# A second matrix product cut into seven block products: z = h wo1 on pairs of 512-token blocks, with the gated sums' second half moved into the first gated pair

## The chip, the cores and the metric

The program runs on one core of one Trainium2 chip. The metric is device time in microseconds (us) of one execution. Before the change three runs gave 1319.36, 1319.44 and 1320.01 us, median 1319.44 us.

The engines are named as in the profile: PE is TensorE (matrix products), PEld its weight loads, DVE is VectorE, ACT is ScalarE, POOL is GpSimd, and SP is the engine that issues every DMA of this program.

## The reference, cut to what matters

```python
def _attn_ref(q, k, v):                 # q, k, v: 8 x 8 heads x 576 x 64
    scores = scale * np.matmul(q, k.transpose(0, 1, 3, 2))
    ret = scores * Dmat[None]           # decay, lower triangle
    return np.matmul(ret, v)
def _moe_ref(x, w1, w2, w3, w_out):     # x: 4608 x 512, w1..w3: 512 x 768, w_out: 768 x 512
    h = np.maximum(np.maximum(x @ w1, x @ w2), x @ w3)
    return (h @ w_out)
def _moe2_ref(x, w1, w2, w3, w_out):    # w1, w2: 512 x 1024, w3: 1024 x 1024, w_out: 1024 x 512
    a = x @ w1
    b = x @ w2
    h = a * b @ w3
    return (h @ w_out)
```

The output is `_moe2_ref(_moe_ref(_attn_ref(q, k, v)))` for 4608 tokens.

## The kernel before, in words

Every matrix product is made in three matmuls. A float32 operand is **split** into a rounded half (`copy_r`, on ACT) and the rest (`low`, a subtraction on DVE or POOL), and the product of two split operands is high by high, low by high and high by low. The helper `product` writes these three for each pair of operand pieces into one PSUM bank. A matmul has 128 x 128 weights and up to 512 moving columns.

The stages follow each other on PE:

1. **h** (to 580 us of the trace). Nine blocks of 512 tokens: attention, then `h = max(x w1, x w2, x w3)` with six row groups of 128 (`ps_h`, L416), stored to DRAM in `h_d`. Other weights are turned from float64 words into float32 on the way and parked in DRAM (`wo1_d`, `wp_d`, `wo2_d`, `w3t_d`). What runs when is a list of due times: `when(t, ...)` counts in units of one `ps_h` product, `T_BLK = 18` units make a block, and `t_last` is the start of the ninth block. In that block the next stage's weights are fetched and split.
2. **z = h wo1** (581 to 732 us). Twelve tiles of `N2 = 384` tokens; for each, six pieces of 128 along the inner dimension (`KF1`) by four output groups (`KD`), three matmuls each. `load_h` and `split_h` fetch and split h pieces into `hh` and `hl` (a ring of four, the `low` on DVE and POOL in turn). The four banks of a tile go through `zo` to `z_d`. In `slots` of this loop stand steps of the next stages: `sums_of` makes the seven sums of blocks of the gated weights (`a11` to `s4`) for two operands `i` and two column halves `q`, and `open_34` fetches the weights of stage 3.
3. **w4 = w3 w_out** (732 to 776 us), a weight product. For each of eight output groups `m`, eight pieces `k` into one bank (`ps_w`, L584). `wo2` is wholly resident; the `w3t` pieces come through three buffers `raw34`.
4. **gated** (776 to 1122 us). Six pairs of token tiles; in each, four column blocks `o`, and per column block seven block products on the sums (`X`, `V`, `Y` banks; `snap` copies a bank on ACT, `plus` adds on DVE, `times` multiplies on POOL). Two operand sets `ops[0]` and `ops[1]` serve the pairs in turn; `operands` fetches `zr` and makes the next pair's differences and splits in between.
5. **out** (to 1317 us): the product with w4, also by seven block products.

The order of instructions on an engine is the order in which the code calls them. Each engine takes its own queue strictly in that order; SP too, so a DMA whose buffer is not free yet holds all DMAs behind it.

Of the kernel before, what the change touches and what calls it, by code (L numbers as in the profile page):

```python
# [21 lines left out]
G = H // 2  # L22
# [65 lines left out]
def tile_retention_maxout_bilinear(ctx: ExitStack, tc, a, out):  # L88
# [20 lines left out]
    z_d = [dram.tile([P, KD, N2], F32, name=f"z_d{t}") for t in range(NT // N2)]  # L109
# [103 lines left out]
    def w3_unit(t, j, half):  # L213
# [39 lines left out]
    def x_tiles(t):  # L253
        if t not in xs:
            xs[t] = (x_p.tile([P, G, N1], F32R, tag="xh", name="xh"), x_p.tile([P, G, N1], F32R, tag="xl", name="xl"))
# [199 lines left out]
    def open_z():  # L455
        right.close()
        cv_x.close()
        p = zp["p"] = bx.enter_context(tc.tile_pool(name="zp", bufs=1, side="right"))
        zp["w"] = [(p.tile([P, DM], F32R, name=f"w1oh{k}"), p.tile([P, DM], F32R, name=f"w1ol{k}")) for k in range(KF1)]
# [11 lines left out]
    def get_w1o(k):  # L471
        return splitter(zp["p"], wo1_d[:, k], *zp["w"][k], nc.vector if k % 2 else nc.gpsimd, "wr", 2)

    H_RING, H_AHEAD = 4, 4
    hq = dict(loaded=0, split=0)

    def load_h():
        n = hq["loaded"]
        if n < n2 * KF1:
            hq["loaded"] = n + 1  # L480
            j, k = divmod(n, KF1)
            raw = hq[n] = zp["p"].tile([P, N2], F32, tag="hr", name="hr", bufs=H_AHEAD)
            t0, done = j * N2, 0
            while done < N2:
                blk, off = divmod(t0 + done, N1)
                m = min(N1 - off, N2 - done)
                load(raw[:, done:done + m], h_d[blk][:, k, off:off + m])
                done += m

    def split_h():  # L490
        n = hq["split"]
        if n < n2 * KF1:
            hq["split"] = n + 1
            raw = hq.pop(n)
# [506 lines left out]
```

## Time and profile before

| what | us |
|---|---|
| median of three runs | 1319.44 |
| the profiled execution, device time | 1319.27 |
| its span, first to last instruction | 1317.5 |
| PE busy | 1298.2 |
| stage z on PE, first matmul to the first of w4 | 150.9 |
| stage w4 on PE | 43.6 |
| DVE busy in stage z | 75.8 |
| POOL busy in stage z | 74.3 |

The device time is 1.8 us more than the span. A busy PE in the table is PE with a matmul in its pipe. The views used below are the page's own parts, the instructions of one tile, the chain of work that ended last in order of time, the busy time in stretches, the groups of equal instructions, who waited for whom, the DMA issues and the timeline of one engine. In the timeline a row gives start, duration, engine, line, operation and, in brackets, the idle time before it.

### The profile page before, as it was taken

How to read it: one execution, taken by the hardware profiler on the slowest of the kernel's cores; microseconds unless marked ns; L12 is line 12 of the kernel's file. 1: busy time of each engine (PE TensorE's matmuls, PEld its weight loads, DVE VectorE, ACT ScalarE, POOL GpSimd, SP SyncE). 2: the span in 40 equal slices, each digit the busy share in tenths (PEclk: the TensorE clock that was granted, in tenths of full speed). 3: DMA queues.
4: the chain of work that ended last, by engine and by line, in shares of the span. 5: the costliest groups of instructions: out<-in, count | busy, mean ns of one | idle time of the engine just before them, and what ended most of it. 6: DMA issues, size and time to landing. Idle time of an engine off the chain costs nothing.

```text
span 1317.5 us, 24536 instructions
## 1 busy us (share of the span) xinstructions
PE 1298.2 (99%) x9464; PEld 1185.1 (90%) x9464; DVE 757.7 (58%) x1134; ACT 448.5 (34%) x878; POOL 402.2 (31%) x356
## 2 busy tenths in 40 slices
PE   7999999999999999999999999999999999999998
PEld 5888888888888878889999899999999999999998
DVE  5995656766668575227644334334333437788885
ACT  3541212222222122114434333333333324455553
POOL 2111111111111110026634334333433434544443
PEclk9999999999999999999999999999999999999999
DMA  9964768877779885237557432222222222544552
GB/s 219 246 141 97 178 154 211 203 192 192 194 174 188 166 177 132 92 104 226 182 185 235 145 123 85 72 79 74 89 97 79 72 94 73 179 154 152 167 157 93
DMA packets 347748, 193.53 MB, mean 147 GB/s; under 512 B 243056, under 2 KB 321392, under 8 KB 347632
## 3 DMA queue, kind: packets, MB, share of 16 engines
q1 hardware_dynamic: 347632, 191.97, 53.9%
q8 instruction: 74, 1.21, 0.4%
q14 instruction: 42, 0.34, 0.1%
HBM read 125.85 MB, written 66.06 MB: 146 GB/s over the span
## 4 chain that ended last, share of the span: by engine, by line
PE 88%; SPq 6%; DMA 3%; issue 1%; DVE 1%; POOL 0%; ACT 0%; DVEq 0%; POOLq 0%; ACTq 0%
PE ps_h L416 30%; PE ps_x L584 23%; PE ps_y L584 11%; PE ps_z L584 9%; SPq L99 6%; PE ps_v L584 6%; PE ps_w L584 3%; PE o L334 2%; PE sc L321 2%; PE st L346 1%; PE o L340 1%; DMA kn<-in_k_dram 1%; DMA z_d<-zo 0%; DMA w<-w_d 0%; DMA raw<-in_moe_w_dram 0%
## 5 line engine op out<-in xcount | busy, mean ns | idle before, releaser
L416 PE MATMUL ps_h<-xh,w1h 128*128 128x512 f32 (+1 forms) x664 | 259.1, 392 | 0.6 <-ACT hb L93 0.5
L416 PE MATMUL ps_h<-xh,w1l 128*128 128x512 f32 (+1 forms) x664 | 254.6, 385 | 0.4 <-DVE w1l L96 0.2
L416 PE MATMUL ps_h<-xl,w1h 128*128 128x512 f32 (+1 forms) x664 | 174.1, 384 | 0.0
L416 PEld LDWEIGHTS ps_h<-xh,w1h 128*128 128x128 f32 x664 | 124.6, 188 | 30.9 <-issue 3.6
L416 PEld LDWEIGHTS ps_h<-xh,w1l 128*128 128x128 f32 x664 | 124.7, 188 | 24.7 <-DVE w1l L96 0.7
L416 PEld LDWEIGHTS ps_h<-xl,w1h 128*128 128x128 f32 x664 | 123.0, 188 | 24.8
L310 POOL TENSOR_TENSOR v<-v,tables 128x512 f32<-128x512 f32 x40 | 44.5, 1113 | 327.6 <-DMA v<-in_v_dram 306.6
L426 DVE TENSOR_TENSOR hb<-ps_h,hb 128x512 f32<-128x512 f32 (+1 forms) x110 | 74.4, 677 | 112.4 <-PE ps_h L416 104.6
L880 POOL TENSOR_TENSOR c<-c 128x384 f32<-128x384 f32 x72 | 81.7, 1134 | 175.4 <-DVE c L748 87.5
L743 ACT ACTIVATE snap<-ps_x 128x384 f32<-128x384 f32 x120 | 58.5, 492 | 190.7 <-PE ps_x L584 188.5
L584 PE MATMUL ps_z<-hh,w1oh 128*128 128x384 f32 x288 | 96.3, 334 | 0.8 <-issue 0.8
L584 PE MATMUL ps_z<-hl,w1oh 128*128 128x384 f32 x288 | 96.4, 335 | 0.6 <-DVE hl L96 0.6
L584 PE MATMUL ps_z<-hh,w1ol 128*128 128x384 f32 x288 | 96.2, 334 | 0.0
L158 ACT ACTIVATE e<-raw 128x512 f32<-128x512 f32 x64 | 42.8, 669 | 154.4 <-DMA raw<-in_moe_w_dram 96.9
L93 ACT ACTIVATE hb<-ps_h 128x512 f32<-128x512 f32 (+1 forms) x56 | 32.5, 580 | 176.4 <-PE ps_h L416 176.4
L96 POOL TENSOR_TENSOR hl<-hr,hh 128x384 fp32r<-128x384 f32 x36 | 39.4, 1093 | 78.0 <-ACT hh L93 74.2
L748 DVE TENSOR_TENSOR c<-ps_v,snap 128x384 f32<-128x384 f32 x48 | 26.6, 557 | 61.6 <-PE ps_v L584 39.6
L307 POOL TENSOR_TENSOR q<-q,tables 128x512 f32<-128x512 f32 (+1 forms) x31 | 32.0, 1032 | 94.3 <-DMA q<-in_q_dram 76.4
L328 DVE TENSOR_TENSOR p<-sc,tables 128x512 f32<-128x512 f32 (+1 forms) x80 | 47.1, 628 | 18.6 <-PE sc L321 18.6
L93 ACT ACTIVATE hh<-hr 128x384 fp32r<-128x384 f32 x72 | 36.1, 522 | 56.9 <-PE ps_z L584 30.5
L584 PEld LDWEIGHTS ps_z<-hh,w1oh 128*128 128x128 f32 x288 | 54.1, 188 | 1.2 <-issue 1.2
L584 PEld LDWEIGHTS ps_z<-hl,w1oh 128*128 128x128 f32 x288 | 54.1, 188 | 1.1 <-DVE hl L96 1.1
(215 smaller groups left out, 3360.0 us busy)
## 6 DMA issues: line engine op xcount, KB each, us to landing
g_d<-c SPq DMA_DIRECT2D x96, 192.0 KB, 1.9
raw<-in_moe_w_dram SPq DMA_DIRECT2D x34, 512.0 KB, 5.8
h_d<-hb SPq DMA_DIRECT2D x54, 256.0 KB, 3.1
gr<-g_d SPq DMA_DIRECT2D x12, 1024.0 KB, 6.2
z_d<-zo SPq DMA_DIRECT2D x12, 768.0 KB, 3.6
zr<-z_d SPq DMA_DIRECT2D x48, 192.0 KB, 3.3
out_dram<-ob SPq DMA_DIRECT2D x36, 256.0 KB, 2.0
v<-in_v_dram SPq DMA_DIRECT2D x32, 256.0 KB, 4.7
```

The lines of the kernel that those rows point to most:

```text
L93: nc.scalar.activation(dst, src, AF.Copy)
L96: eng.tensor_tensor(dst, full, hi.bitcast(F32), ALU.subtract)
L99: nc.sync.dma_start(out=dst, in_=src)
L158: nc.scalar.activation(z["e"], raw[:, :, 1].bitcast(F32), AF.Copy, scale=2.0 ** -112)
L307: nc.gpsimd.tensor_tensor(z["q"][:, :r], z["q"][:, :r], qs[:, j, :r].unsqueeze(3).to_broadcast([P, r, G, 32]), ALU.mult)
L310: nc.gpsimd.tensor_tensor(z["v"], z["v"], vd.unsqueeze(2).to_broadcast([P, H, D]), ALU.mult)
L328: nc.vector.tensor_tensor(z[g][:c, :, :c], z["sc"][g][:c, :, :c], mask[:c, :c].unsqueeze(1).to_broadcast([c, G, c]), ALU.mult)
L416: nc.tensor.matmul(ps[:, cols], l, r, start=n == 0, stop=n == len(mms) - 1)
L426: nc.vector.tensor_tensor(hb, ps[:, cols], hb, ALU.max)
L584: nc.tensor.matmul(ps, l, r, start=start and j == 0, stop=stop and j == len(mms) - 1, skip_group_check=again)
L743: nc.scalar.activation(t, ps[:, :N2], AF.Copy)
L880: nc.gpsimd.tensor_tensor(x, x, y, ALU.mult)
```

## The change

**z by seven block products.** Tokens are taken in pairs of 512-token blocks (`z_groups`: four pairs, and the ninth block as two halves of 256). The output's four groups are two halves, the inner dimension's six pieces are two halves of three (`KH`). The seven sums of wo1's blocks are made in the ninth block by `z_weights`, from two loads per piece. The differences of the four blocks of h are made per group on DVE (`sub_h`), on 1536 columns at once, and each of the seven resulting operands is split whole: one ACT copy and one DVE subtraction of 1536 columns. Before, each split was of 384 columns. Sums of products leave PSUM through `zs` (ACT) and a DVE addition into `zo`, and `z_d` now holds pairs of tiles.

**The gated sums.** Only half `q = 0` is made beside z, all its `low` on DVE; half `q = 1` is made in the first two column blocks of the first gated pair (`more`, called by `tick`). That pair makes the next pair's operands in its last two column blocks instead of in all four.

**w4.** The loop now runs over `k` outside, with eight banks open; `wo2` is no longer resident but comes through `raw34` too, one piece for every two of `w3t`. The `low` of w3t is on DVE alone, that of wo2 on DVE and POOL in turn.

Places of tiles: `x` has one pool per block; the second half of the gated sums lies on the right side. The transposed w3 is stored in rows of 512 elements.

```diff
-        zp["w"] = [(p.tile([P, DM], F32R, name=f"w1oh{k}"), p.tile([P, DM], F32R, name=f"w1ol{k}")) for k in range(KF1)]
+        zp["w"] = {x: [p.tile([P, KH, half], F32R, name=f"z{x}{v}") for v in "hl"] for x in AN}
...
+    Z_ORDER = (("a11", "b11"), ("a12", "b21"), ("s2", "t2"), ("s1", "t1"), ("s3", "t3"), ("s4", "b22"), ("a22", "t4"))
+    Z_RING = 3
+    z_groups = [(2 * j, 2 * j + 1, 0, N1) for j in range(n_blk // 2)] + [(n_blk - 1, n_blk - 1, N1 // 2, N1 // 2)]
...
+    def sub_h(eng, j, dst, x, y, tag=None):
+        if j < len(z_groups):
+            r = hr[j, dst] = raw_h(tag)[:, :, :z_groups[j][3]] if tag else hr[j, x if x[0] == "b" and dst == "t1" else y]
+            eng.tensor_tensor(r, hr[j, x], hr[j, y], ALU.subtract)
...
+    def split_h(n):
+        j, n = divmod(n, len(Z_ORDER))
+        if j < len(z_groups):
+            x = Z_ORDER[n][1]
+            raw, size = hr[j, x], z_groups[j][3]
+            hh, hl = hq[j, n] = [zp["p"].tile([P, KH, N1], F32R, tag=f"h{v}", name=f"h{v}", bufs=Z_RING)[:, :, :size] for v in "hl"]
             copy_r(hh, raw)
-            low(nc.vector if n % 2 else nc.gpsimd, hl, raw, hh)
+            low(nc.vector, hl, raw, hh)
...
+        behind_z = {0: [(h_t4, 0)], 1: [(load_h, 1, "b12")], 2: [(load_h, 1, "b21")], 3: [(h_t3, 1), (load_h, 2, "b22")],
+                    4: [(h_t1, 1)], 5: [(h_t2, 1), (load_h, 2, "b11")], 6: []}
+        for j, (_, _, _, size) in enumerate(z_groups):
...
+            for n, (x, y) in enumerate(Z_ORDER):
+                bank_of = "XVXYXYX"[n]
...
+                for i in range(2):
+                    ms = slice(i * P, i * P + P)
+                    product(ps[i][:, :size], [(ah[:, c, ms], al[:, c, ms], bh[:, c], bl[:, c]) for c in range(KH)], fresh, True, not fresh)
+                for i in range(2):
+                    if n in (0, 2, 3):
+                        saved[n, i] = snap_z(ps[i], size)
+                    elif n == 6:
+                        keep_z(j, 2 + i, 0, ps[i])
+                    else:
+                        keep_z(j, *{1: (i, 0), 4: (2 + i, 1), 5: (i, 1)}[n], ps[i], saved.pop(({1: 0, 4: 3, 5: 2}[n], i)))
+                split_h(j * len(Z_ORDER) + n + Z_RING)
+                for fn, dj, *args in behind_z[n]:
+                    fn(j + dj, *args)
+                if steps and n in (2, 3, 5, 6):
                     steps.pop(0)()
...
-        for m in range(KF2):
-            th, tl = w3t.pop(m)
-            ps = bank8("ps_w")
-            product(ps, [(th[:, k], tl[:, k], oh[k], ol[k]) for k in range(KF2)])
...
+        for n in range(2 * KF2):
+            k, e = divmod(n, 2)
+            th, tl = w3t.pop(n)
+            for m in range(4 * e, 4 * e + 4):
+                if k == 0:
+                    ps_w.append(bank8(f"ps_w{m}"))
+                product(ps_w[m], [(th[:, m % 4], tl[:, m % 4], *wo2[k])], k == 0, k == KF2 - 1)
...
+            prepare_34(*[(get_w3t, n + 3)] * (n + 3 < 2 * KF2), *[(get_wo2, k + 2)] * (e == 1 and k + 2 < KF2))
...
+        more = in_turn([sums_of(i, 1, lambda: mp, 2, (nc.vector, nc.vector)) for i in range(2)])
+        more.pop(0)()
...
+                if p == 0 and o == 2:
+                    for step in steps:
+                        step()
+                    open_second()
+                    a1, b1 = (operands(1, ops[1], c) for c in range(2))
+                    steps = [a1[0], waiting, waiting, *a1[1:], b1[0], waiting, *b1[1:]]
```

In stage z, DVE's queue held before, around the end of a tile, splits of 384 columns (`hl`), the gated weights' sums (`s3`, `s4` and their rest) and copies out of PSUM (`zo`):

```order
L96 TENSOR_TENSOR hl_6697<-hr_6607,hh_6696 128x384
L96 TENSOR_TENSOR hl_6741<-hr_6656,hh_6740 128x384
L558 TENSOR_TENSOR s3_6748<-a00_6466,a10_6470 128x512
L631 COPY zo_6750<-ps_z_6619 128x384
L631 COPY zo_6750<-ps_z_6621 128x384
L96 TENSOR_TENSOR hl_6791<-hr_6700,hh_6790 128x384
L96 TENSOR_TENSOR s2l10_6310<-s2_6682,s2h10_6309 128x512
```

Now, behind the fourth, fifth and sixth product of the first group, it holds splits of 1536 columns, the next group's differences (`T3`, `b12`, `T2`), gated sums and additions out of PSUM:

```order
L96 TENSOR_TENSOR hl_6481<-T2_6236,hh_6480 128x1536
L522 TENSOR_TENSOR T3_6484<-b22_6163,b12_6418 128x1536
L96 TENSOR_TENSOR a22l00_6330<-a11_6454,a22h00_6329 128x512
L606 TENSOR_TENSOR a11_6454<-a10_6452,a11_6454 128x512
L676 TENSOR_TENSOR zo_6509<-ps_X0_6359,zs_6476 128x512
L676 TENSOR_TENSOR zo_6513<-ps_X1_6360,zs_6478 128x512
L96 TENSOR_TENSOR hl_6518<-b11_6277,hh_6517 128x1536
L522 TENSOR_TENSOR b12_6418<-b12_6418,b11_6277 128x1536
L676 TENSOR_TENSOR zo_6540<-ps_Y0_6456,zs_6438 128x512
L676 TENSOR_TENSOR zo_6544<-ps_Y1_6457,zs_6440 128x512
```

All of h's splits and differences have moved to DVE, four times as wide, and POOL has none of them left.

SP's queue in stage w4 was, before, pairs of w3t loads with a store of a finished bank between them:

```order
L99 DMA raw34_8044<-w3t_d_61 128x512
L99 DMA raw34_8046<-w3t_d_61 128x512
L99 DMA w4_d_97<-w4_8048 128x512
L99 DMA raw34_8089<-w3t_d_61 128x512
L99 DMA raw34_8091<-w3t_d_61 128x512
L99 DMA w4_d_97<-w4_8093 128x512
```

Now there is a wo2 load among every two of w3t, all through the same three buffers, and the stores come at the stage's end:

```order
L99 DMA raw34_7552<-w3t_d_61 128x512
L99 DMA zr_7554<-z_d0_73 128x768 x2
L99 DMA raw34_7577<-w3t_d_61 128x512
L99 DMA raw34_7581<-wo2_d_60 128x512
L99 DMA raw34_7601<-w3t_d_61 128x512
L99 DMA raw34_7623<-w3t_d_61 128x512
L99 DMA raw34_7627<-wo2_d_60 128x512
```

Three loads now belong to 24 matmuls of PE, where two did.

In the first column block of the first gated pair, DVE's queue was, before, the additions out of PSUM (`c`) with a difference now and then:

```order
L748 TENSOR_TENSOR c_8366<-ps_v0_8334,snap_8350 128x384
L748 TENSOR_TENSOR c_8368<-ps_v1_8335,snap_8352 128x384
L748 TENSOR_TENSOR c_8421<-ps_x0_8332,snap_8399 128x384
L748 TENSOR_TENSOR c_8423<-ps_x1_8333,snap_8401 128x384
L678 TENSOR_TENSOR t_8428<-zr_8403 128x384
```

Now six operations of the gated sums stand between the first two pairs of additions:

```order
L830 TENSOR_TENSOR c_7970<-ps_v1_7937,snap_7954 128x384
L96 TENSOR_TENSOR a22l01_7488<-a11_7932,a22h01_7487 128x512
L606 TENSOR_TENSOR a11_7932<-a10_7930,a11_7932 128x512
L96 TENSOR_TENSOR a11l01_7484<-a00_7926,a11h01_7483 128x512
L606 TENSOR_TENSOR a10_7930<-a00_7926,a10_7930 128x512
L96 TENSOR_TENSOR s1l01_7490<-a11_7932,s1h01_7489 128x512
L606 TENSOR_TENSOR a00_7926<-a11_7932,a00_7926 128x512
L830 TENSOR_TENSOR c_8035<-ps_x0_7934,snap_8007 128x384
```

The second pair of additions, which PE needs before its seventh product, has moved behind them.

## Rows read from the trace of the kernel before

**Rows 1.** The page, busy time by engine, and by slice PE and its clock.

```profile
PE 1298.2 (99%) x9464; PEld 1185.1 (90%) x9464; DVE 757.7 (58%) x1134; ACT 448.5 (34%) x878; POOL 402.2 (31%) x356
...
PE   7999999999999999999999999999999999999998
...
PEclk9999999999999999999999999999999999999999
```

**Rows 2.** Who waited for whom on PE: us in total, times, longest.

```profile
PE ps_x L584 <- DVE c L748: 2.4, 1, 2.4
...
PE ps_z L584 <- issue: 0.8, 1, 0.8
```

**Rows 3.** Tiles ps_z and ps_w: ns min/median/max of one, first and last start.

```profile
L584 PE MATMUL ps_z<-hh,w1oh x288: 334/334/414, 581.4 to 731.8; 128*128 128x384 f32 x144
...
L584 PE MATMUL ps_w<-oh,th x64: 387/389/393, 732.3 to 775.2; 128*128 128x512 f32 x64
```

**Rows 4.** The chain in order of time: start, us, what and how many.

```profile
609.80 122.67 PE ps_z L584 x706
732.47 43.56 PE ps_w L584 x192
...
780.28 2.12 PE ps_x L584 x12
...
839.57 2.08 PE ps_x L584 x12
...
1190.88 2.85 PE ps_x L584 x24
```

**Rows 5.** Busy time in the stretches of z and w4: length, then engine by engine.

```profile
581.40:732.30 150.90, 150.33 (x864) 149.78 (x865) 75.82 (x88) 65.08 (x132) 74.25 (x60) 1.00 0.61 195
733.00:775.00 42.00, 42.00 (x187) 34.75 (x186) 18.16 (x19) 16.68 (x33) 19.23 (x16) 1.00 0.55 176
```

**Rows 6.** Timeline of DVE in the ninth block and at the start of z.

```profile
545.28 0.69 DVE L426 TENSOR_TENSOR hb<-ps_h,hb 128x512 f32<-128x512 f32 x1 [4.80 <-PE ps_h L416]
545.89 0.68 DVE L96 TENSOR_TENSOR w1ol<-wr,w1oh 128x512 fp32r<-128x512 f32 x1
...
581.20 0.55 DVE L96 TENSOR_TENSOR hl<-hr,hh 128x384 fp32r<-128x384 f32 x1
```

**Rows 7.** Timeline of DVE and of POOL in stage w4.

```profile
739.29 1.26 DVE L96 TENSOR_TENSOR tl<-raw,th 128x512 fp32r<-128x512 f32 x1 [6.22 <-ACT th L93]
...
738.71 1.29 POOL L96 TENSOR_TENSOR tl<-raw,th 128x512 fp32r<-128x512 f32 x1 [13.86 <-ACT th L93]
```

**Rows 8.** ACT's copies by form: busy, mean ns of one, idle before.

```profile
L93 ACT ACTIVATE hb<-ps_h 128x512 f32<-128x512 f32 x52 | 30.9, 595 | 173.1 <-PE ps_h L416 173.1
...
L93 ACT ACTIVATE hh<-hr 128x384 fp32r<-128x384 f32 x72 | 36.1, 522 | 56.9 <-PE ps_z L584 30.5 <-DMA hr<-h_d 10.3 <-issue 8.7
```

**Rows 9.** DMA issues, 733 to 765 us: count, KB each, median us to landing.

```profile
raw<-w3t_d SPq DMA_DIRECT2D x12, 256.0 KB, 4.0
```

**Rows 10.** DMA issues of the whole run, the same columns.

```profile
raw<-in_moe_w_dram SPq DMA_DIRECT2D x34, 512.0 KB, 5.8
...
gr<-g_d SPq DMA_DIRECT2D x12, 1024.0 KB, 6.2
...
a<-wp_d SPq DMA_DIRECT2D x16, 256.0 KB, 4.4
...
raw<-wo_d SPq DMA_DIRECT2D x8, 256.0 KB, 3.3
```

**Rows 11.** The gated stage's additions on DVE and multiplications on POOL, by form.

```profile
L880 POOL TENSOR_TENSOR c<-c 128x384 f32<-128x384 f32 x72 | 81.7, 1134 | 175.4 <-DVE c L748 87.5 <-issue 51.8 <-PE ps_x L584 21.2
...
L748 DVE TENSOR_TENSOR c<-ps_v,snap 128x384 f32<-128x384 f32 x48 | 26.6, 557 | 61.6 <-PE ps_v L584 39.6 <-ACT snap L743 22.0
```

More of the change, by code (lines that the diff above doesn't have):

```diff
@@ L469, in splitter @@
         return split
[L471 to L488, printed above, removed]
@@ L510, in tile_retention_maxout_bilinear @@
-    for n in range(2):
-        when(t_last + 15 + n, split_h)
+    for c, tag in enumerate(("T3", "T2", "b21")):
+        for n, step in enumerate(z_weights(c, tag)):
+            when(t_last + 0.5 + 3 * c + (1.2 + 0.35 * n if n else 0), step)
+    for n, x in enumerate(("b12", "b22", "b11")):
+        when(t_last + 1 + 2 * n, load_h, 0, x)
+    when(t_last + 10.5, load_h, 0, "b21")
+    when(t_last + 9, load_h, 1, "b22")
+    for n, fn in enumerate((h_t3, h_t1, h_t2)):
+        when(t_last + 9.5 + 1.6 * n, fn, 0)
@@ L513, in tile_retention_maxout_bilinear @@
+    for n in range(Z_RING):
+        when(t_last + 13.6 + n, split_h, n)
+    when(t_last + 15.2, load_h, 1, "b11")
     with tc.manual_schedule():
@@ new lines, in snap_z, with keep_z @@
+        def snap_z(ps, size):
+            t = zo_p.tile([P, N1], F32, tag="zs", name="zs", bufs=6)[:, :size]
+            nc.scalar.activation(t, ps[:, :size], AF.Copy)
+            return t
+        def keep_z(j, m, n, ps, other=None):
+            t, off, size = z_groups[j][n], n * z_groups[j][2], z_groups[j][3]
+            o = zo_p.tile([P, N1], F32, tag="zo", name="zo", bufs=4)[:, :size]
+            if other is None:
+                nc.scalar.activation(o, ps[:, :size], AF.Copy)
+            else:
+                nc.vector.tensor_tensor(o, ps[:, :size], other, ALU.add)
+            at0, done = t * N1 + off, 0
+            while done < size:
+                pair, to = divmod(at0 + done, 2 * N2)
+                part = min(2 * N2 - to, size - done)
+                load(z_d[pair][:, m, to:to + part], o[:, done:done + part])
+                done += part
@@ L862, in next_steps, with tick @@
             def next_steps(n):
-                for _ in range(n if p + 1 < n_pair or o < 1 else 2 * n):
+                for _ in range(0 if p == 0 else n if p + 1 < n_pair or o < 1 else 2 * n):
+                    if steps:
+                        steps.pop(0)()
+            def tick(n=1):
+                for _ in range(n if p == 0 else 0):
                     if steps:
```

239 lines of the change are left out of this document (133 added, 106 removed).

## The prediction

> **What bounds the kernel now.** I read the page first: PE is busy 1298.2 of 1317.5 us, in nine tenths or more of every slice but the first and the last, at a granted clock of nine tenths or more, which is the 2.4 GHz level [rows 1]. So time is PE's, and anything else counts only where PE waits for it. PE's waits are few: the longest beside the start is 2.4 us, and in stage z the gap at its beginning of 0.8 us [rows 2]. Then I read the stage that changes. Its first matmul starts at 581.4 us and the first of w4 at 732.3 us, so z holds PE for 150.9 us [rows 3]. In it DVE is busy for 75.8 us and POOL for 74.3 us of 150.9 us [rows 5]: half idle, and off the path. A second is thus gained where PE has fewer columns to stream, and lost where an engine that was half idle becomes late.
>
> **PE's work in z.** From the chain, 706 matmuls of 384 columns take 122.67 us, 0.1738 us each; 192 of 512 columns take 43.56 us, 0.2269 us each; 24 of 256 columns take 2.85 us, 0.1188 us each [rows 4]. Before, 12 tiles x 6 pieces x 4 groups x 3 matmuls = 864 of 384 columns: 150.1 us, and 150.9 us as measured, with the small gaps. After, a group has 7 products x 2 halves x 3 pieces x 3 matmuls = 126. Four groups are of 512 columns (504 matmuls, 114.3 us) and one of 256 (126 matmuls, 15.0 us). The sum is 129.3 us. PE loses **21.6 us** of work.
>
> The rows let the size be checked. 384, 512 and 256 columns at 2.4 GHz are 160, 213.3 and 106.7 ns; each row is 12 to 14 ns above. The Trainium skill, "TensorE: Matmul & The Clock Gate", section "Wait — 56ns, not 53.3ns?", has a fixed cost of about 2.5 ns per warm matmul; with it the gain would be 17.9 us as an estimate (41,472 columns fewer, and 234 matmuls fewer at 2.5 ns). The rows above don't agree with so small a cost.
>
> **What feeds z.** Each full group lasts 126 x 0.2269 = 28.6 us, a product 4.08 us. Does DVE keep up, now that POOL has no part in it? No row has an operation of 1536 columns. The rest of a split takes 0.55 us for 384 columns and 0.68 us for 512, and the next operation follows 0.61 us after the start of one of 512 [rows 6]. So 128 columns cost 0.13 us, 1536 columns 0.68 + 8 x 0.13 = 1.72 us; three spacings of 0.61 us, 1.83 us, bound it from above. I take 1.7 us. A group has 7 rests and 4 differences (18.7 us), 6 additions out of PSUM (3.7 us at 0.61), and a quarter of the 22 operations of the gated sums (3.4 us): 25.8 of 28.6 us. It fits, at nine tenths. ACT has per group 7 copies of 1536 columns, 8 of 512 and some of the sums; with 0.52 us for 384 and 0.60 for 512 [rows 8] one of 1536 is about 1.2 us, and the sum about 17 us.
>
> The load is uneven: behind products 4, 5 and 6 DVE has 4.6, 4.6 and 5.8 us of work in 4.08 us, and 2.9 to 3.3 us behind the others. Its worst lag is so some 2.7 us, plus 1.2 to 2 us for ACT's copy ahead of the rest. A split is made two products (8.2 us) before PE needs it, so nothing is late here, by some 2 us. The weights' 33 operations of 256 columns and the first differences fall into the ninth block, where DVE is busy one operation in 2.7 us. **Start of z: 0**, with the old gap of 0.8 us staying.
>
> The h loads are of 768 KB; the nearest rows are 512 KB in 5.8 us and 1024 KB in 6.2 us [rows 10]. Each is issued at least 7 us before its use, b12 the closest; I take 0 for them.
>
> The last group of 256 columns runs at 2.14 us a product. Behind its fourth product two rests of w4's weights wait on a DMA of 256 KB (4.0 us in the next stage, [rows 9]), and the additions that free X for the seventh product stand behind them on DVE. **0.3 us**, bounds 0 and 2.
>
> **w4.** PE's 192 matmuls stay. But three buffers now carry three loads per 5.45 us of PE (24 matmuls) instead of two. A buffer's round is landing 4.0 us [rows 9], ACT's copy 0.6 us, and the rest on POOL 1.3 us or on DVE 0.7 to 1.3 us (1.26 beside a busy POOL, [rows 7]): 5.3 to 5.9 us. At 5.9 it slips 0.45 us in each of seven rounds, 3.2 us, of which a lead of some 1.2 us at the start takes its part: **2.0 us**. Lower bound 0 (loads in 3.3 us [rows 10], round 4.6); upper 12.6 us (loads in the 5.8 us of the 512 KB row, round 7.7 us at POOL's price and 7.3 at DVE's, so some 2 us in each of seven rounds, less the lead).
>
> **First gated pair.** A column block takes 7 x 2.12 = 14.84 us of PE [rows 4]. DVE has in it 7 additions at 0.56 us [rows 11] and now 11 operations of the sums at 0.61 us, 10.6 us; where POOL runs one of its three multiplications (1.13 us, [rows 11]) DVE's own stands still, as the 1.26 us for 0.68 show [rows 7]: up to 3.4 us more, 14.0 us. In the first block the sums also wait for their load, issued after w4's stores and 4.4 us on its way [rows 10], some 2.6 us beyond their place. The lag of 1.8 us reaches the bank that the next block's second product needs: **1.2 us**, bounds 0 and 5.8 (all 22 operations at 1.26 us). The next pair's operands, squeezed into two blocks, have their DMA started 4 us or more ahead: 0.
>
> One more thing has a price but no direction. Twelve matmuls take 2.12 us in the pairs with one operand set and 2.08 us in those with the other [rows 4], and the moved half of the sums changes which tiles meet. Six of 24 blocks may gain 0.28 us each, six may lose as much: 0, bounds -1.7 and +1.7 us.
>
> What hides at nothing: ACT's copies, z's stores (256 KB where they were 768 KB, as many bytes), and the moved load steps on SP.
>
> **Sum.** 1319.27 - 21.6 + 0.3 + 2.0 + 1.2 = **1301.2 us**. That is against the profiled execution, which is 0.17 us under the median.
>
> **Rivals.**
> - *DVE becomes the bound of z.* It does from (28.6 - 7.1) / 11 = 1.95 us per operation of 1536 columns. At 2.1 us a group takes 30.2 us, the stage 137 us, the total about 1309 us. For it: DVE is at nine tenths, and the same operation took 1.26 us beside POOL [rows 7]. Against it: POOL has nothing in this stage.
> - The Trainium skill, "VectorE: DVE Perf Modes", sections "The TRN2 errata" and "The DRAIN you can't avoid", has (N + 151) / 0.96 ns for an fp32 addition and no overlap of one operation with the next: as an estimate 1.76 us for 1536 columns and 27.3 us a group, still under 28.6. The duration agrees with the 0.68 us row, the spacing of 0.61 us doesn't.
> - *The same, and slower than before.* The five groups then take over 150.9 us, from 4 (11p + 7.1) + 5.5p + 5.5 = 150.9, p = 2.36 us. At the stretched price of 1.26 us per 512 columns, 3.8 us, a group takes 49 us and the total is near 1386 us. What decides is whether DVE streams 1536 columns of two SBUF operands as freely as 512.
> - *w4's buffers*: the upper bound above, about 1312 us.
> - *Matmuls at 2.5 ns over their columns*, a gain of 17.9 us only: 1305 us.
> - *The change doesn't do what it says*: excluded for PE's part, since its queue is 234 matmuls shorter in the order of instructions.
>
> **How the numbers follow.** Forecast 77% (1296 to 1306); w4's buffers 8% (1306 to 1314); DVE as bound, still faster, 6% (1304 to 1316); smaller gain per matmul 3%; slower 4%; something that leaves it within 0.2% of before, 2%. The range 1296 to 1310 leaves out the upper parts of the second and third and the last two, less than 2 in 10. About 0.2%, 2.6 us, is what a measurement of this kernel can tell from no change. Faster 94%, same 2%, slower 4%.
>
> **What would show it.** In the changed profile: z's matmuls at 0.227 us each from about 581 to 711 us, 630 of them, with no wait on DVE's `hl`; DVE's operations of 1536 columns at 1.7 us (wrong from 1.95); w4 at 43.6 us plus some 2 us of waits for `tl` or `ol`; a wait of PE in the first gated pair on DVE's `c`, once or twice; all pairs from the second on as before. A w4 stage over 50 us would prove the buffers' rival, a group over 29 us DVE's.

## The result, and the profile after

| | before | after |
|---|---|---|
| device time, median of four runs, us | 1319.72 | 1297.42 (1295.95 to 1300.0) |
| the profiled execution: device time, span | 1319.27, 1317.5 | 1296.76, 1294.8 |
| ratio after to before | | 0.9828, 95% interval 0.9807 to 0.9850 |

The forecast was 1301.2 us in a range from 1296 to 1310 us. The time lies in the range, 3.8 us under the forecast. The profiled execution is 0.7 us faster than the median; its profile tells where the forecast and the time part. The page of the changed kernel answers to [rows 1]:

```profile
PE 1274.6 (98%) x9230; PEld 1141.9 (88%) x9230; DVE 828.0 (64%) x1217; ACT 474.6 (37%) x872; POOL 323.2 (25%) x289
...
PEclk9999999999999999999999999999999999999999
```

PE has 234 matmuls fewer, is busy 23.6 us less (1298.2 before), and still sets the time; its granted clock is at the 2.4 GHz level in every slice. DVE has 70 us more to do than before, POOL 79 us less. The busy time in the stretches of z, w4, and the first half and the second half of the first gated pair (length, then PE, PEld, DVE, ACT, POOL, clock, DMA share, GB/s) answers to [rows 5]:

```profile
580.60:710.10 129.50, 129.50 (x630) 109.68 (x631) 106.16 (x104) 71.00 (x88) 0.00 (x0) 1.00 0.51 169
710.10:754.40 44.30, 43.83 (x194) 35.99 (x193) 22.70 (x29) 22.27 (x42) 16.25 (x13) 1.00 0.61 192
754.40:784.90 30.50, 30.24 (x170) 29.57 (x170) 21.13 (x35) 15.15 (x31) 7.76 (x7) 1.00 0.41 136
784.90:814.00 29.10, 29.10 (x169) 29.10 (x169) 14.88 (x25) 11.66 (x27) 15.20 (x14) 1.00 0.34 116
```

Stage z holds PE for 129.5 us instead of 150.9 us [rows 3], with no idle in it. DVE is busy in 106 of 129.5 us where it was in 76 of 150.9. In the third row PE is short of its stretch by 0.3 us, in w4 by 0.5 us. The chain in order of time (start, us, what, how many) gives the pitches, as [rows 4] did:

```profile
633.97 8.16 PE ps_X L637 x36
642.13 4.08 PE ps_V L637 x18
...
699.48 2.16 PE ps_X L637 x18
...
776.32 2.12 PE ps_y L637 x12
...
787.13 2.08 PE ps_v L637 x12
...
876.67 2.12 PE ps_x L637 x12
...
906.27 2.08 PE ps_x L637 x12
```

A product of 18 matmuls of 512 columns takes 4.08 us, 226.7 ns each; one of 256 columns takes 2.16 us, 120.0 ns each. In the gated stage a pair that uses the first operand set (776, 876 us) begins at 2.12 us per twelve matmuls and goes on at 2.08 us (787, 906 us): its last two column blocks, whose sums the change has moved to the right side, run faster. Before, all four ran at 2.12 us.

By PE's own stage boundaries, in us (the last column is a second execution of the changed kernel, of the run "changed" below):

| stage | before | after | second execution |
|---|---|---|---|
| z starts at | 581.4 | 580.6 | 582.4 |
| z | 150.9 | 129.5 | 129.8 |
| w4 | 43.6 | 44.3 | 44.1 |
| gated, 23 of 24 column blocks | 338.8 | 337.8 | 338.7 |
| last block and out | 199.4 | 199.2 | 199.1 |

So of 22.7 us of span, 21.4 are z's, w4 gives 0.8 back, the gated stage gains 1.7 by its pitch and loses 0.8 in the first pair, and h and the end have 1.1 us less. The second execution gains less (1299.4 us of device time): h is 1.0 us longer there than before, and the first pair loses 1.6 us.

### The profile page after: what moved, and what is told of

Its sections match the earlier page's. It is cut to its first block, busy times and chain, and to the rows that moved or that the text cites. A ratio compares the mean times of both kernels' runs of the same rounds, so it can differ in the third digit from the quotient of the medians.

```text
span 1294.8 us, 23828 instructions
## 1 busy us (share of the span) xinstructions
PE 1274.6 (98%) x9230; PEld 1141.9 (88%) x9230; DVE 828.0 (64%) x1217; ACT 474.6 (37%) x872; POOL 323.2 (25%) x289
## 4 chain that ended last, share of the span: by engine, by line
PE 95%; DVE 2%; DMA 1%; issue 1%; ACT 0%; POOL 0%; SPq 0%; POOLq 0%; DVEq 0%; ACTq 0%
PE ps_h L417 34%; PE ps_x L637 23%; PE ps_y L637 11%; PE ps_X L637 6%; PE ps_v L637 5%; PE ps_Y L637 3%; PE ps_w L637 3%; PE o L335 3%; PE sc L322 3%; PE st L347 2%; PE ps_V L637 1%; PE o L341 1%; DMA w<-w_d 0%; DMA a<-wp_d 0%; DMA q<-in_q_dram 0%
## 5 line engine op out<-in xcount | busy, mean ns | idle before, releaser
L311 POOL TENSOR_TENSOR v<-v,tables 128x512 f32<-128x512 f32 x40 | 44.3, 1107 | 322.6 <-DMA v<-in_v_dram 311.4
L96 POOL TENSOR_TENSOR ol<-raw,oh 128x512 fp32r<-128x512 f32 x4 | 5.6, 1408 | 216.6 <-DMA z_d<-zo 212.7
L165 DVE CUSTOM_DVE_ANT_0 m<-m,r 128x1024 uint16<-128x1024 uint16 x64 | 51.4, 804 | 7.0 <-ACT r L160 0.2
L830 DVE TENSOR_TENSOR c<-ps_x,snap 128x384 f32<-128x384 f32 x48 | 25.4, 552 | 43.6 <-PE ps_x L637 43.6
L169 DVE SCALAR_TENSOR_TENSOR w<-raw,m 128x512 int32<-128x512 int32 x64 | 49.4, 774 | 0.5
L93 ACT ACTIVATE xh<-o 128x512 fp32r<-128x512 f32 (+1 forms) x40 | 22.1, 553 | 73.4 <-PE o L341 60.7
L315 DVE STREAM_TRANSPOSE qt<-q 128x512 f32<-128x512 f32 (+1 forms) x31 | 29.9, 966 | 21.1 <-issue 6.3
L322 PE MATMUL sc<-qt,kt 64*64 64x128 f32 (+1 forms) x1152 | 40.6, 266 | 2.7 <-DVE p L329 1.0
```

Source lines behind the costliest of these rows:

```text
L93: nc.scalar.activation(dst, src, AF.Copy)
L165: nc.vector.tensor_tensor(z["m"], z["m"], z["r"], ALU.add)
L169: nc.vector.scalar_tensor_tensor(w, z["hi"], -0x80000000, z["m"], ALU.bitwise_and, ALU.bitwise_or)
L311: nc.gpsimd.tensor_tensor(z["v"], z["v"], vd.unsqueeze(2).to_broadcast([P, H, D]), ALU.mult)
L322: nc.tensor.matmul(z["sc"][g][keys, h, :c], z["kt"][rows, h, keys], z["qt"][rows, h, :c], start=True, stop=True)
L830: nc.vector.tensor_tensor(r, ps[:, :N2], t, ALU.add)
```

## The experiments

Edits are against the changed kernel, if not said otherwise. Stage times are PE's, from first matmul to first matmul of the next stage.

### Does DVE hide in z by its sum? Runs "dve1" and "dve5"

```diff
             low(nc.vector, hl, raw, hh)
+            if size == N1 and n in (2,):
+                low(nc.vector, hl, raw, hh)
```

In dve5 the list is (0, 1, 2, 3, 4). The splits 0 to 2 of the first group are made before z, so that three of the added operations fall into z in dve1 (107 operations of DVE for 104) and 17 in dve5 (121).

dve1: 

> In each full group of stage z one of the seven splits makes its rest on DVE twice (the same 1536 columns written again): 1.67 us of DVE more per group. Theory A: a group costs DVE 25.4 to 26.1 us of PE's 28.6 us, so one operation more (27.1 to 27.8 us) still hides: z stays at 129.5 to 129.8 us. Rival B: what counts is not the sum but the load behind single products, where DVE is behind already: then z grows by up to 1.7 us per group, to as much as 136 us.

dve5: 

> In each full group of stage z five of the seven splits make their rest on DVE twice: 8.35 us of DVE more per group, 33.8 to 34.5 us of work against PE's 28.6 us. Theory A: DVE then sets the pace, with a lead of a few us used up first: over the four full groups some 12 to 20 us more, z at 141 to 150 us, and PE waits for DVE's hl behind nearly every product. Rival B: the splits, made two products ahead, hide it: z stays under 132 us.

Busy time of dve1 in z and of dve5 in z, the same columns as above:

```profile
582.70:714.30 131.60, 130.55 (x630) 109.44 (x631) 111.23 (x107) 70.98 (x88) 0.00 (x0) 1.00 0.50 166
```

```profile
582.00:736.00 154.00, 138.26 (x631) 112.11 (x632) 135.73 (x121) 70.72 (x88) 0.00 (x0) 0.97 0.43 142
```

dve1: z takes 131.6 us, 2.1 us more, some 0.7 us for each of the three operations, and the run 1301.8 us. Theory A wanted at most 0.3 us; rival B, up to 6.7. The truth lies between: the sum of DVE's work has room (111 of 131.6 us busy), but the place where the operation was added, behind the seventh product of a group, has only about 1.67 - 0.7 = 1.0 us of it. PE's waits show `hl` three times, the longest 0.6 us, where the changed kernel shows none. Other places were not tried with one operation.

dve5: z takes 154.0 us, 24.5 us more and 3.1 us more than before the change, and the run 1322.9 us. DVE is busy 135.7 of 154 us. PE's longest entry of waits, and two stretches of 20 us:

```profile
PE ps_X L639 <- DVE hl L96: 10.3, 6, 1.9
```

```profile
620.00:640.00 20.00, 16.88 (x65) 12.79 (x64) 19.48 (x16) 11.39 (x13) 0.00 (x0) 0.91 0.46 159
660.00:680.00 20.00, 16.89 (x73) 13.63 (x74) 19.90 (x18) 9.95 (x12) 0.00 (x0) 1.00 0.38 126
```

Theory A holds, with its size too low (12 to 20 us): in the second to fourth group DVE is hardly ever idle and PE waits for it. Some of PE's own time grew as well, by 8.8 us of busy time. In part that is the granted clock: it is 0.91 from 620 to 640 us, where some of the stretch is at the 1.2 GHz level and 65 matmuls fit, and 1.00 from 660 to 680 us, where 73 fit beside as much idle time. Over z it is 0.97 on average; by an estimate 0.03 of 154 us, some 5 of the 8.8 us. The rest is not explained.

### Why POOL had to go: run "zpool"

```diff
-            low(nc.vector, hl, raw, hh)
+            low(nc.vector if n % 2 else nc.gpsimd, hl, raw, hh)
```

> In stage z every second rest of h's splits is made on POOL instead of on DVE, as the kernel before did with its splits of 384 columns; the same work, on two engines. Theory A: DVE and POOL stand in each other's way on operations with two operands in SBUF (in w4 a rest of 512 columns took 1.26 us beside POOL's, 0.68 us alone). A rest of 1536 columns on POOL is then about 3 x 1.15 = 3.5 us, 3.5 of them per group 12 us, in which DVE's own operations of 1536 columns take up to 5 us; PE waits for hl, and z becomes 3 to 20 us longer. Rival B: two engines share the work freely: DVE falls to some 19.7 of 28.6 us per group, its operations stay at 1.75 us, PE waits for nothing, z stays at 129.5 us.

z takes 145.8 us, 16.3 us more, and the run 1317.1 us: nearly all of the change's gain is gone. Operations by form in z (count, busy, mean ns of one, idle before them):

```profile
L96 POOL TENSOR_TENSOR hl<-T,hh 128x1536 fp32r<-128x1536 f32 x11 | 39.6, 3601 | 72.0 <-ACT hh L93 37.8 <-PE ps_X L637 34.2
L96 DVE TENSOR_TENSOR hl<-b,hh 128x1536 fp32r<-128x1536 f32 x11 | 22.5, 2050 | 13.6 <-PE ps_Y L637 7.1 <-PE ps_V L637 6.5
```

Two of POOL's rests with DVE's operations beside them (start, duration):

```profile
607.88 3.52 POOL L96 TENSOR_TENSOR hl<-b,hh 128x1536 fp32r<-128x1536 f32 x1 [1.30 <-ACT hh L93]
619.15 3.50 POOL L96 TENSOR_TENSOR hl<-T,hh 128x1536 fp32r<-128x1536 f32 x1 [7.75 <-ACT hh L93]
```

```profile
607.80 1.28 DVE L676 TENSOR_TENSOR zo<-ps_X,zs 128x512 f32<-128x512 f32 x2
609.00 4.02 DVE L522 TENSOR_TENSOR b<-b,b 128x1536 f32<-128x1536 f32 x1
...
619.63 3.58 DVE L96 TENSOR_TENSOR s1l<-a,s1h 128x512 fp32r<-128x512 f32 x1 [0.87 <-ACT s1h L93]
```

PE's waits in the same stage, and the busy time of the stretch in which the longest fell:

```profile
PE ps_X L637 <- DVE zo L676: 9.5, 4, 4.4
```

```profile
640.00:670.00 30.00, 25.61 (x102) 20.64 (x101) 23.90 (x18) 14.00 (x17) 10.30 (x3) 0.89 0.55 187
```

An operation of 1536 columns takes POOL 3.6 us. A DVE operation with both operands in SBUF that starts while POOL runs ends only after POOL's: the difference at 609.00 us takes 4.02 us instead of 1.75 and ends 1.6 us after POOL, the rest of 512 columns at 619.63 us takes 3.58 us instead of 0.68 and ends 0.6 us after POOL. The two additions `zo` at 607.80 us, with one operand in PSUM, take 1.28 us together beside POOL, no longer than alone. The 2.05 us is the average of operations that met POOL and others that did not. PE then waits for DVE's additions `zo`, queued behind the operations that stood, up to 4.4 us at a time, and the granted clock is 0.89 in the stretch from 640 to 670 us, part of it at the 1.2 GHz level. The Trainium skill, "SBUF — State Buffer", section "SBUF: two separate sides", has DVE operations with two SBUF inputs and POOL's exclude each other for a whole instruction; this run agrees (3.58 us instead of 0.68 us for the DVE operation at 619.63 us). Half of z's rests on a second engine cost more than all of them on one.

### Who is late in the first gated pair: run "wait"

```diff
         more.pop(0)()
+        more.insert(0, waiting)
```

> In the first gated pair every step of the sums' second half comes one place later (an empty step stands ahead of them), so that ACT meets the first copy a22h, which waits for its load, later. Theory A: PE's loss in the first column block (15.36 us for 14.84 us) comes from ACT, whose copy out of PSUM (snap) stood behind a22h, and not from DVE's amount of work; then the first block goes to 14.9 us and the second, with the same DVE work, stays within 15.1 us, -0.5 us in all. Rival B: DVE's 22 operations are what is late; then the loss of 0.8 us stays and only moves to the second block.

First what the changed kernel shows. ACT in the first column block (start, duration, idle before), and the chain there:

```profile
756.76 0.49 ACT L825 ACTIVATE snap<-ps_x 128x384 f32<-128x384 f32 x1 [0.51 <-PE ps_x L637]
762.27 0.63 ACT L93 ACTIVATE a22h<-a 128x512 fp32r<-128x512 f32 x1 [5.02 <-DMA a<-wp_d]
762.81 0.85 ACT L825 ACTIVATE snap<-ps_x 128x384 f32<-128x384 f32 x2
```

```profile
757.60 4.65 DMA a<-wp_d
...
762.27 0.63 ACT a22h L93
762.90 0.39 ACT snap L825
...
763.33 2.39 PE ps_x L637 x12
```

The load of the sums is issued at 757.60 us and lands 4.65 us later. ACT stands 5.02 us for it with the copy `a22h` at the head of its queue; the two copies `snap` out of X, which PE needs before its next product into X, are behind it. In the run "wait" (1297.6 us in all) the blocks take 15.04 and 14.96 us (15.36 and 15.09 before the edit, 14.84 without a wait): the loss falls from 0.8 to 0.3 us, and no wait of PE is listed in the first pair. DVE, with the same 22 operations, is busy in 21 of the 30.5 us of the two blocks in the changed kernel. One execution's loss alone would show little: in nine executions of kernels without it the loss goes from 0.5 to 1.8 us, and with the edit it is 0.3 us here, 0.8 in "best" and 0.5 in "shift5" (below). What tells the two apart is PE's list of waits: eight of the nine have a wait for ACT's `snap` there, of 0.3 to 1.1 us ("zpool" has none), and none of the three with the edit has one. So most of the loss was ACT's queue and the load; some 0.2 us in the second block stays open. The loss was larger where the load took longer: in the execution of "changed" it took 5.50 us,

```profile
759.43 5.50 DMA a<-wp_d
```

and the two blocks 16.21 and 15.10 us, a loss of 1.6 us.

### What is lost in w4: runs "raw4" and "rows512"

```diff
-            return splitter(t34["p"], wo2_d[:, k], *wo2[k], nc.gpsimd if k % 2 else nc.vector, "raw34", 3)
+            return splitter(t34["p"], wo2_d[:, k], *wo2[k], nc.gpsimd if k % 2 else nc.vector, "raw34", 4)
...
-            t = zo_p.tile([P, N1], F32, tag="zs", name="zs", bufs=6)[:, :size]
+            t = zo_p.tile([P, N1], F32, tag="zs", name="zs", bufs=5)[:, :size]
```

The load of w3t has the same edit.

> The ring raw34 of stage w4 has four buffers instead of three (one buffer of zs in stage z is given up for it). Theory A: what w4 lost (44.3 us for 192 x 0.2269 = 43.6 us) is a ring that is one load short at its start; then w4 takes 43.6 to 43.8 us, -0.5 to -0.7 us. Rival B: the loss comes from the entry into w4, where POOL's ol is late (0.5 us) because its load waits behind z's last stores on SP; then more buffers give nothing, 44.3 us. z stays at 129.5 us in both.

w4 takes 44.4 us, as with three buffers, and the run 1299.7 us; rival B. In the changed kernel's timeline PE's only listed wait in w4 is at its start, and SP's queue ahead of it shows why (SPq rows: the issue of a DMA, how many):

```profile
716.68 0.50 PE L637 MATMUL ps_w<-ol,th 128*128 128x512 f32 x1 [0.47 <-POOL ol L96]
```

```profile
707.51 1.79 SPq L99 DMA_DIRECT2D z_d<-zo  x4
709.40 0.39 SPq L99 DMA_DIRECT2D raw<-w3t_d  x1
709.88 0.39 SPq L99 DMA_DIRECT2D raw<-wo_d  x1
```

The load of wo2's second piece is issued at 709.88 us, behind four stores of z that wait for their additions; POOL's rest of it then starts at 715.34 us, and PE stands for it. Issuing w4's first loads two products earlier (run "best", below) takes the loss away: 43.55 us. In the executions without that edit w4 took 44.0 to 44.7 us, whatever else was edited.

The other run undoes the storage of w3 in rows of 2 KB:

```diff
-            load(w3t_d[:, j, 4 * half:4 * half + 4], wt.rearrange("p (m i) -> p m i", i=P))
+            load(w3t_d[:, 4 * half:4 * half + 4, j, :], wt.rearrange("p (m i) -> p m i", i=P))
...
-            return splitter(t34["p"], flat(w3t_d[:, k, 4 * e:4 * e + 4]), *map(flat, w3t[n]), nc.vector, "raw34", 3)
+            return splitter(t34["p"], w3t_d[:, 4 * e:4 * e + 4, k, :], *map(flat, w3t[n]), nc.vector, "raw34", 3)
```

> The transposed w3 is parked in DRAM as before the change: each store of 256 KB writes rows of 512 B, and now each load of w4 reads rows of 512 B too; nothing else is changed. Theory A: the 1.8 us that stage h gained at 470 us (PE's wait of 1.4 us for DVE's xl and of 0.5 us for ACT's hb, both gone) came from the store in rows of 2 KB, since DVE's transpose stood 9.12 us for the store's landing before and 5.11 us after. Then both waits come back and z starts 1.5 to 2 us later, at about 582.3 us. Rival B: they went because x has a pool for each block; then z still starts at 580.6 us. For w4: if a buffer's round (landing, ACT's copy of 0.63 us, DVE's rest of 0.68 us) sets the pace, loads that land in over 4.1 us make the stage longer than 44.3 us, by about 8 x (landing - 4.1) us; if PE alone sets it, the stage stays at 44.3 us.

The run took 1300.0 us. w4 takes 44.7 us, 0.35 us more; in "wait", whose w4 is not edited, it took 44.6 us, so the difference shows nothing. z starts at 582.1 us, 1.5 us later, with PE's wait of 1.3 us for `xl` back. That looked like theory A for stage h. But the same wait is back in "raw4" too, which stores rows of 2 KB, and in "changed", which is the changed kernel itself. PE's waits of the two in stage h:

```profile
PE o L335 <- DVE xl L96: 1.3, 1, 1.3
```

```profile
PE o L335 <- DVE xl L96: 1.2, 1, 1.2
```

The first execution of the changed kernel has no such wait. DVE stood for the landing of the store of `w3t` for 5.1 us there and for 8.6 us in "raw4". So neither theory is shown. In the executions whose code up to z is the changed kernel's, but for a split or two, z starts at 580.6, 581.2, 582.0, 582.4, 582.7, 583.1 and 584.4 us; one execution's h stage differs from the next by as much as the 0.8 us in question, and what the change does to it stays open: from 0.8 us less to 3.0 us more than the 581.4 us before. As to the loads: at the median they land in 2.8 us (2.9 us in rows of 512 B), not in 4.0 us:

```profile
raw<-w3t_d SPq DMA_DIRECT2D x13, 256.0 KB, 2.8
```

### Why twelve gated matmuls take 2.12 or 2.08 us: runs "align", "pad352", "shift5"

"align" and "pad352" put one unused tile at the top of the right side, of 32 or 352 bytes, so that all tiles of that side move down:

```diff
+    pad = ctx.enter_context(tc.tile_pool(name="pad", bufs=1, side="right")).tile([P, 8], F32, name="pad")
+    nc.gpsimd.memset(pad, 0.0)
```

In "pad352" the tile is [P, 88].

align: 

> A tile of 32 bytes is put at the top of the right side of SBUF, so that every tile on that side starts 32 bytes lower: at a multiple of 64 bytes, as the tiles on the left do, instead of 32 bytes above one. Nothing else is changed. Theory A: twelve gated matmuls take 2.12 us where moving and stationary tiles stand differently to 64 bytes (operand set 0 on the right against sums on the left) and 2.08 us else; then the six column blocks at 14.84 us and more go to 14.56 us, -1.7 us, and in the out stage the even steps go from 10.01 to 9.92 us, -0.8 us, in all about 1294.3 us for 1296.8 us. Rival B: it is the side, or which tiles share a stretch of SBUF; then all pitches stay and the time stays at 1296.8 us.

The run took 1299.0 us. Theory A fell, and rival B as well: the first pair's blocks went from 2.12 to 2.08 us as expected, but the last two blocks of the second operand set went the other way. The chain of "align":

```profile
839.79 2.08 PE ps_y L639 x12
841.87 4.20 PE ps_x L639 x24
846.07 2.12 PE ps_v L639 x12
...
875.71 2.08 PE ps_v L639 x12
```

pad352: 

> A tile of 352 bytes instead of 32 is put at the top of the right side of SBUF: all tiles of z, of the gated stage and of the out stage then start at the same place within 512 bytes, on either side. Theory C (formed after the 32 bytes, which made the slow pairs of tiles fast and others slow): what counts is how far apart the moving and the stationary tile start, within 512 bytes; 0, 160 and 320 bytes gave 2.08 us for twelve gated matmuls, 192 and 352 bytes gave 2.12 us. With 0 bytes everywhere all gated column blocks take 14.56 us beside waits and the even out steps 9.92 us: -1.7 and -0.8 us against the changed kernel, stage by stage. Rival B: the pitch goes by something else (a place within a larger stretch, other engines' traffic); then some of blocks 9, 10, 17 and 18 or others stay at 14.84 us.

All gated blocks ran at 14.56 us beside waits, blocks 9, 10, 17 and 18 too: theory C held there. But every out step, of 84 matmuls of 256 columns, now took 10.08 us, where odd and even steps had taken 9.92 and 10.01:

```profile
776.30 2.08 PE ps_x L639 x12
...
1153.90 1.44 PE ps_v L639 x12
```

1.44 us for twelve is 120.0 ns. So for 256 columns another distance than 0 is better, and the run as a whole gained nothing (1301.1 us).

shift5: 

> Only places and two positions in the order are changed. Empty tiles move the tiles so that a moving tile starts 160 bytes (within 512) beyond its stationary tile in stages h, z, w4 and out, and 0 bytes beyond it in the gated stage; the sums' steps in the first gated pair come one place later (as in the run 'wait'); the first loads of w4 are issued behind the first product of z's last group instead of behind the third. Theory D, from the rows so far: 256 columns take 120.0 ns at 0 bytes and 117.4 ns at 160 (from 10.08 us per out step with 0 everywhere, and 10.01 and 9.92 where the two alternate); 384 columns take 173.3 ns at 0 and at 160 and 176.7 ns at 192 and 352. Then all out steps take 9.86 us (-1.9 us), all gated blocks 14.56 us beside waits (-1.7 us), the first pair gains 0.4 us, w4 0.5 us: together -4.5 us against the changed kernel by stages. For 512 columns there is no row at 160: like 384 they stay at 226.7 ns; like 256 they fall by 2.6 ns, h by 5 us, z by 1.3 us, w4 by 0.5 us. Rival E: the pitch goes by other engines' accesses; then out stays near 10 us a step and gated blocks at 14.84 us turn up elsewhere.

The edit is a row of such unused tiles (for h, z, w4, and the two buffers of out), with the tile of 352 bytes of "pad352" and the two changes of order shown under "best":

```diff
+    left.enter_context(tc.tile_pool(name="padx", bufs=1, side="left")).tile([P, 40], F32, name="padx")
     x_p = {2: left.enter_context(tc.tile_pool(name="x2", bufs=1, side="left"))}
...
         zp["w"] = {x: [p.tile([P, KH, half], F32R, name=f"z{x}{v}") for v in "hl"] for x in AN}
+        p.tile([P, 40], F32, name="padz")
...
+            if k == 0:
+                t34["p"].tile([P, 40], F32, name="padw", bufs=1)
             wo2[k] = [t34["p"].tile([P, DM], F32R, tag=x, name=x) for x in ("oh", "ol")]
...
                 opx.close()
+                ctx.enter_context(tc.tile_pool(name="pada", bufs=1, side="right")).tile([P, 40], F32, name="pada")
...
+        ctx.enter_context(tc.tile_pool(name="padb", bufs=1, side="left")).tile([P, 88], F32, name="padb")
         gpool[1] = gp = ctx.enter_context(tc.tile_pool(name="gb", bufs=1, side="left"))
```

The run took 1311.9 us, 14.5 us more than the changed kernel's median. The chain in z, in its last group of 256 columns, and in w4:

```profile
627.46 4.22 PE ps_V L640 x18
...
716.03 2.11 PE ps_X L640 x18
```

```profile
726.50:771.40 44.90, 44.90 (x193) 36.09 (x192) 23.32 (x28) 20.75 (x40) 14.78 (x13) 1.00 0.55 176
```

With the moving tile 160 bytes beyond the stationary one, 512 columns take 234.3 ns on average (4.22 us for 18) instead of 226.7: z 132.9 us, w4 45.0 us without any wait, and z starts at 593.5 us instead of 580.6 us. 256 columns take 117.3 ns in z instead of 120.0. Theory D was right for 256 columns in z and for the gated stage (all blocks at 14.56 us beside waits), wrong for 512 columns, for which neither of its two cases came, and wrong for out, where each step took 9.97 us and not 9.86.

### A version that beats both, and before with the same places: runs "best", "changed", "before_pad"

"best" has the 352 bytes, the 160 bytes ahead of the out stage's right buffer, and two changes of order; "before_pad" is the kernel before the change with these two unused tiles alone:

```diff
+    ctx.enter_context(tc.tile_pool(name="pad", bufs=1, side="right")).tile([P, 88], F32, name="pad")
...
-                if steps and n in (2, 3, 5, 6):
+                if steps and n in ((2, 3, 5, 6) if j < 4 else (0, 2, 3, 5)):
...
+        more.insert(0, waiting)
...
                 opx.close()
+                ctx.enter_context(tc.tile_pool(name="pada", bufs=1, side="right")).tile([P, 40], F32, name="pada")
```

best: 

> The changed kernel with all tiles of the right side moved down by 352 bytes, so that moving and stationary tiles stand 0 bytes apart (within 512) in h, z, w4 and the gated stage, and with the right one of the out stage's two operand buffers left 160 bytes apart as it was; the sums' steps of the first gated pair one place later; w4's first loads two products earlier. From the rows of the single runs: gated blocks all at 14.56 us beside waits, -1.7 us; first pair -0.3 us; w4 at 43.6 us, -0.7 us; out stage unchanged at 10.01 and 9.92 us. Together -2.7 us against the changed kernel of the same call. If the pitches go by something else than the distance of the tiles, -1.0 us or less.

changed: 

> The changed kernel itself, beside 'best' and 'before_pad' on one chip: 1296 to 1300 us, z at 129.5 us, w4 at 44.3 us; stage h ends anywhere from 580 to 584 us, as it did in the runs so far, whatever was edited.

before_pad: 

> The kernel before the change with the same 352 bytes ahead of the right side and the out buffer left where it was in relation to its partner. If the distance of the tiles sets the pitch, all 24 gated blocks of before go to 14.56 us, 12 of them from 14.84: -3.4 us, about 1316 us for 1319.4. Then the 1.7 us that the change gained in the gated stage belong to places of tiles that before could have had as well, and block products, sums and w4 alone give 1316.0 - 1294.7 = 21.3 us. If it doesn't, before stays at 1319.4 us.

All on one chip, with ten runs of before at 1320.27 us:

| run | median, us | ratio to before, 95% interval | w4 | 23 gated blocks |
|---|---|---|---|---|
| best | 1296.49 | 0.9816 (0.9803 to 0.9830) | 43.55 | 336.1 |
| changed | 1299.45 | 0.9847 (0.9833 to 0.9860) | 44.05 | 338.7 |
| before_pad | 1317.10 | 0.9975 (0.9963 to 0.9986) | 43.56 | 335.4 |

"best" beats the changed kernel by 3.0 us, about as expected (2.7). In the profiled executions 2.6 us are the gated stage's (1.7 by the pitch, 0.9 in the first pair) and 0.5 us w4's; h was 0.8 us longer. w4 of "best", and a row of the first pair of "before_pad":

```profile
712.90:756.40 43.50, 43.50 (x194) 36.03 (x193) 21.75 (x28) 20.85 (x40) 15.29 (x13) 1.00 0.56 182
```

```profile
779.92 2.08 PE ps_x L585 x12
```

In w4 PE has no idle left. Before itself gains 3.2 us from the places of its tiles alone, with all 24 blocks at the faster pitch beside waits. So the 1.7 us that the change gained in the gated stage come from where its tiles happen to lie. With the places made equal, "before_pad" and "best" differ by 20.6 us; by an estimate from the two differences above, some 1.4 us of these belong to the two changes of order in "best".

## Why the prediction was right, step by step

- **PE's work in z: right.** Forecast 129.3 us for 630 matmuls, measured 129.5; the rows gave 226.9 and 118.8 ns, and the changed kernel 226.7 and 120.0 ns. The 2.5 ns per matmul that the Trainium skill has in "TensorE: Matmul & The Clock Gate", section "Wait — 56ns, not 53.3ns?", are not what these matmuls show: 226.7 is 13.4 ns over 512 columns at 2.4 GHz, 173.3 over 384 as much, 120.0 over 256 13.3.
- **DVE keeps up: right, with a smaller margin than said.** An operation of 1536 columns takes 1.75 us and the next follows after 1.67 (forecast 1.7):

```profile
610.03 1.75 DVE L96 TENSOR_TENSOR hl<-b,hh 128x1536 fp32r<-128x1536 f32 x1
611.70 1.75 DVE L522 TENSOR_TENSOR T<-b,b 128x1536 f32<-128x1536 f32 x1
613.36 0.69 DVE L96 TENSOR_TENSOR a11l<-a,a11h 128x512 fp32r<-128x512 f32 x1
```

  In the second to fourth group DVE is busy 26.2, 25.3 and 26.9 of 28.6 us (forecast 25.8); the row of the fourth:

```profile
666.40:695.00 28.60, 28.60 (x127) 23.66 (x127) 26.87 (x28) 15.28 (x19) 0.00 (x0) 1.00 0.43 139
```

  The margin is not "some 2 us" but about 1.0 at the one place tried (dve1). The rival on DVE was near: one operation more in a group already makes PE wait, five make z longer than before the change (dve5), and POOL beside DVE costs 16 us (zpool); that POOL has nothing in this stage was named as what speaks against it. The total that the forecast gave for the slowest case, "near 1386 us", does not follow from its own formula, which gives 222 us for z and so some 1390 us; nothing else rests on it.
- **w4: +2.0 forecast, +0.8 and +0.5 measured. The failed step is the landing of the loads.** The 4.0 us of [rows 9] is a median over loads that met other transfers and loads that did not. In the kernel before, the loads from 745 to 757 us, issued in the same pairs but with no load of `zr` ahead of them, landed in 3.0 us at the median; in the changed kernel those from 733.5 to 739 us, beside two loads of `zr`, took 4.6 us:

```profile
raw<-w3t_d SPq DMA_DIRECT2D x5, 256.0 KB, 3.0
```

```profile
raw<-w3t_d SPq DMA_DIRECT2D x2, 256.0 KB, 4.6
```

  Over all of w4 the median is 2.8 us now; no run tests this cause by itself. A buffer's round is then 2.8 + 0.63 + 0.69 = 4.1 us, under the 5.45 us of PE's, and no wait of PE within the stage is listed. What was lost instead is in the main at the entry (0.5 of the 0.8 us is the wait for `ol`), by the loads' place behind z's stores on SP. The forecast had put that trouble inside z, as the last group's 0.3 us; there it cost nothing.
- **First gated pair: +1.2 forecast, +0.8 and +1.6 measured in two executions.** The size was right, by luck in part, as the executions scatter from 0.5 to 1.8 us; the engine was not: ACT's `snap` behind a copy that waits for its load, not DVE's lag (DVE was busy 21 of 30.5 us, where 28 were forecast). That load and its 2.6 us beyond their place stood in the forecast, but only DVE was asked what is queued behind.
- **The gated pitch: 0 forecast, -1.7 measured, which is the end of the bounds that were given.** All six blocks that could gain did, and none of the six that could lose lost. The forecast could not tell the direction; that it came out as a gain is luck of the places.
- **h: nothing forecast.** In the profiled execution z started 0.8 us earlier, in six others 0.2 us earlier to 3.0 us later than before; the executions differ by more than any effect that could be shown. The profiled one was the earliest of all, which is luck too.
- **The sum.** -21.4 (z) + 0.8 (w4) + 0.8 (first pair) - 1.7 (pitch) - 0.8 (h) - 0.4 (last blocks, out, rounding) = -22.7 us of span; forecast -18.1. So w4 (1.2 us), the pitch (1.7 us) and h (0.8 us) make most of the difference, and only w4 of these is a price that the forecast had worked out wrongly. In the later set, on one chip, the medians of before and of the changed kernel differ by 20.8 us, which is nearer to the forecast.

## What to carry to other kernels

Where one engine holds the path at 98%, the gain of an edit is its instructions counted times their measured pitch; what has to be worked out with care is whether the engines that take over the rest have room at the worst place, not on average. A median landing time is a price only for loads that meet as many other transfers as that row's did. When a step is moved, ask of every engine it runs on what is queued behind its first waiting instruction: here it was ACT's, while only DVE's was examined.

## What the runs showed of the hardware that was not expected

The pitch of this kernel's matmuls (float32r halves, a new weight tile for each) depends on where the moving and the stationary tile start in SBUF: "before_pad" changes nothing but places, "align" and "pad352" nothing but places and one memset of the unused tile. The distances of the tiles' start addresses, within 512 bytes, are those the kernels were built with; the ns per matmul are from the rows above:

| distance, bytes | 512 columns | 384 columns | 256 columns |
|---|---|---|---|
| 0 | 226.7 | 173.3 | 120.0 |
| 160 | 234.3 | 173.3 | 117.3 (z); 118.7 (out, both buffers at 160) |
| 192 | | 176.7 | |
| 320 | | 173.3 | |
| 352 | | 176.7 | |

In h, whose 1992 matmuls all stood at 0 (1896 of them of 512 columns), z started 12.9 us later with the shift of 160 bytes than in the changed kernel's first execution, and 9.1 us later than in the latest of the others. The distance accounts for every gated block of the kernels run, and for z and w4. Out is left open: with one buffer at 0 and one at 160 its steps took 9.92 and 10.01 us, with both at 0 10.08 us, but with both at 160 9.97 us, where 84 matmuls at 117.4 ns make 9.86. What causes the differences was not found. A second thing: where PE stood again and again, with five more DVE operations per group or with POOL beside DVE, its granted clock was lower as well, 0.97 and 0.98 over z, so that a late engine cost more than the time it was waited for (PE was busy 138.3 and 133.7 us there for the same 630 matmuls that take 129.5). In "dve1", with three waits of 0.6 us or less, it stayed at 1.00.
